# Modulation rows in column strips, one block of a product moved, gelu groups dealt out again, scaled rows stored from another queue

## The chip, the cores and the metric

The kernel runs on one core of a Trainium2 chip. The metric is the device time of one execution in microseconds (us). A core has five engines with instruction streams of their own: TensorE (PE, matrix products), VectorE (DVE), ScalarE (ACT), GpSimd (POOL) and SyncE (SP, which here only starts transfers). Transfers (DMA) are started from the queues of SP, POOL and ACT.

## The reference

The program computes a block with adaptive layer norm, forward and backward (2048 tokens, model width 1024, hidden width 3584, bfloat16 in and out):

```python
mod = (silu(c) @ w_mod).reshape(1, 6, 1, -1)      # six rows of 1024
sa, ca, ga, sb, cb, gb = mod[:, 0], ..., mod[:, 5]
h = layernorm(x) * (1 + ca) + sa
x = x + ga * irfft2(rfft2(h) * (w_r + 1j * w_i))
h = layernorm(x) * (1 + cb) + sb
x = x + gb * (gelu(layernorm(h) @ w1 + b1) @ w2 + b2)
```

Returned are the result (out_0) and, for a given gradient of it, the gradients of x, w_r, w_i, w1 (out_4), b1, w2, b2, c and w_mod (out_9, 1024 x 6144: column block r is silu(c) as a column times the gradient of row r).

## The kernel before, in words

**Stages.** The program runs once through these stages, on a span of 1370.3 us. First come the modulation rows, the layer norm of x and its fold for the Fourier transform; at the same time PE computes blocks of ph = (gb * grad_out) w2^T, the gradient of the hidden layer. Then comes the forward Fourier stage (matrix products with generated cosines), whose last part also makes the layer norms of the MLP. After it the rest of ph, the MLP forward with its gelu (here from some 300 us), then the gradients of w2, of the hidden layer, the backward Fourier stage, and last the gradient of w1.

**Modulation rows.** `mod_block(r, h)` (L277) computes half h (512 columns) of row r on all 128 partitions at once: eight matmuls (L283) of 128 x 512 whose left operand `u_b` holds silu(c) 128 times over, each adding 128 rows of w_mod, and then a cast out of PSUM (L286) on whichever engine the scheduler picks. Rows 1 and 5 are made earlier; the change touches rows 0, 2, 3 and 4, eight halves. They are issued in three groups (2, 3 and 3 halves) inside the loop over early ph blocks (L934). Row 0 (`saf` after a scaling and a fold) is added to the folded x at the end of the first stage (`fbuf<-fbuf,sb_saf`, DVE).

**ph blocks.** ph has 28 blocks `fc` of four parts of eight matmuls (`ph_part`, L543, matmul at L548); each part is cast out of PSUM by `ph_out` (L540) into `pho` or `phr` and stored. `PH_EARLY` = 10 sets how many are computed ahead of the Fourier stage (block 10 is the last), the rest but four half blocks (from `PH_KEEP` = 24) after it, the second halves of those at the head of the MLP plan.

**Layer norm of the MLP.** For each quarter i of the tokens (tiles `xt`, `ct`) DVE or ACT makes mean and variance; `ln_fin` (L473) takes a square root on ACT and a reciprocal on DVE (L475), and the rows are normalised on DVE (L507) or ACT (L514).

**Gelu groups and passes.** The MLP runs over four token blocks b of 512. `z_block(b, g)` makes a group of four hidden chunks: 32 matmuls (L1076, `pz`), four evictions with the bias on ACT (L1079), and the gelu with its derivative: a square (L1083) and two sigmoids (L1087, L1089) on ACT, nine products on DVE. The first of its results is hh (tiles `hhA`, `hhB`, `hhC`, made by `hh<-gt,gt`), written hh0, hh1, ... by the group's number 7b + g. Work tiles `gt` are held in two sets that the groups use in turn. A pass of the second product (`bo_pass`, 16 matmuls at L1130, `pbo`) uses hh of one group with a block of w2; each b has 14 passes, two per group, so pass k of b = 0 is the first to need hh of group k for k under 7. At L1119 four matmuls of one row and at L1149 four matmuls into 32 partitions each start side by side (`tile_position` and partition ranges).

**What sets the order.** A scheduler places every engine's instructions in one list ahead of time, by its own cost estimates and by priorities (`tc.high_priority()`). PE's order at these places is fixed by hand: `ordered()` ties a matmul to the one before, and the list `plan` (L1166) with its table `Z_AT` says in which order gelu groups ("z"), the kept ph halves ("p") and passes ("b") follow one another. `issue_after` and `behind` hold an instruction behind another in the list.

**The last stage.** `gw1_quads` computes the gradient of w1 in four quads c; each finished tile `gwo` is stored to out_4 (L1681), the first eleven of them from POOL's queue, later ones from SP's. Between them `gmod_scaled` (L1291) makes 32 pieces of out_9, each one activation on ACT (L1298, into one of five tiles `otl`) and one store of 256 KB (L1299). The loop at L1858 takes one such step per quarter of a quad and two in its last nine.

Of the kernel before, what the change touches and what calls it, by code (L numbers as in the profile page):

```python
# [17 lines left out]
P = 128  # L18
# [17 lines left out]
def kernel(  # L36
# [36 lines left out]
    def ps_s(name):  # L73
        return psum.tile([P, 512], FP32, tag="s", name=name)
# [191 lines left out]
    def mod_tile():  # L266
        wring[0] += 1
        return reg.tile([P, NDC, KH], BF16, name="wblk", tag=PXT[3 + wring[0] % 3])

    def mod_load(r, h, wblk, eng, parts=1):  # L270
        cb = 2 * r + h
        src = w_mod[:, cb * KH:(cb + 1) * KH].rearrange("(j p) n -> p j n", p=P)
        for k in range(parts):
            js = slice(k * NDC // parts, (k + 1) * NDC // parts)
            eng.dma_start(out=wblk[:, js, :], in_=src[:, js, :])

    def mod_block(r, h, wblk=None):  # L277
        if wblk is None:
            wblk = mod_tile()[:]
            mod_load(r, h, wblk, nc.sync)  # L280
        pm = (ps_s, ps_d)[wring[0] % 2]("pm")
        for jc in range(NDC):
            nc.tensor.matmul(pm[:], lhsT=u_b[:, jc, :], rhs=wblk[:, jc, :], start=(jc == 0), stop=(jc == NDC - 1))  # L283
        dst = MOD_DST[r][:, h * KH:(h + 1) * KH]
        with tc.high_priority():
            nc.any.tensor_copy(out=dst, in_=pm[:])  # L286
        if r in (1, 4):
            nc.vector.tensor_scalar(out=dst, in0=dst, scalar1=1.0, scalar2=None, op0=ALU.add)

    def fold_d(dst, src, tmp):  # L290
# [237 lines left out]
    def ordered():  # L528
        return tc.issue_after(last_pe[0].ins)

    PH_EARLY, PH_KEEP = 10, NFC - 4

    def ph_out(fc, j, pp):
        ph2 = phs[fc % 4]
# [9 lines left out]
    def ph_part(fc, js):  # L544
        for j in js:
            pp = ps_f("pp")
            for cch in range(NDC):
                last_pe[0] = nc.tensor.matmul(pp[:], lhsT=wt[:, fc % 4, cch, :], rhs=gBoT[j][:, cch, :],  # L548
                                              start=(cch == 0), stop=(cch == NDC - 1))
            ph_out(fc, j, pp)  # L550
# [377 lines left out]

    phs.append(reg.tile([P, 4, BW], BF16, name="phr", tag="ph")[:])

    late_mods = [(r, h) for r in (2, 3, 4) for h in range(2)]
    for fc in range(PH_EARLY):
        if fc > 1:
            ph_part(fc, (0, 1, 2, 3))  # L934
        load_w2t(fc + 4)
        if fc == 4:
            with ordered():
                small_rows()
        if fc == 3:
            for h in range(2):  # L940
                with ordered():
                    mod_block(0, h)
            nc.vector.tensor_scalar(out=sar[:, 0], in0=sar[:, 0], scalar1=8.0, scalar2=None, op0=ALU.mult)
            fold_d(saf.rearrange("p (c d) -> p c d", c=1), sar[:, 0], sar[:, 1])
        if fc in (5, 7):
            with ordered():
                for r, h in late_mods[3 * (fc // 2 - 2):3 * (fc // 2 - 1)]:
                    mod_block(r, h)

    ph_part(PH_EARLY, (0, 1, 2, 3))  # L950
    early_pe = last_pe[0]
# [61 lines left out]
    for fc in range(PH_EARLY + 1, NFC):  # L1013
        if fc >= PH_EARLY + 4:
            load_w2t(fc)
            load_w1({14: 2, 27: 5}.get(fc, 0))
# [150 lines left out]
    Z_AT = [{1: ((0, 4),), 2: ((0, 5),), 3: ((0, 6),), 4: ((1, 0),), 6: ((1, 1),), 7: ((1, 2),), 9: ((1, 3),), 10: ((1, 4),),  # L1167
             11: ((1, 5),), 12: ((1, 6),)}]
    Z_AT += [{k: ((b, g),) for g, k in enumerate((0, 2, 4, 7, 9, 11, 12))} for b in (2, 3)] + [{}]
    for b in range(NB):  # L1170
        for k in range(14):
            plan += [("z",) + bg for bg in Z_AT[b].get(k, ())] + [("b", b, k)]
    boq = {}
    for kind, b, g in plan:
        if kind == "z":
# [117 lines left out]
    def gmod_scaled(rows):  # L1293
        for n in range(len(rows) * NDC):
            k, jc = n // NDC, n % NDC
            gw, r = w1g["gw"][n % 5], rows[k]
            with tc.issue_after(w1g["ev"].ins):
                nc.scalar.activation(out=gw, in_=w1g["gr"][k], func=ACT.Identity, scale=u_rt[:, jc:jc + 1])  # L1298
            nc.gpsimd.dma_start(out=out_9[jc * P:(jc + 1) * P, r * D:(r + 1) * D], in_=gw)  # L1299
            yield  # L1300

    step_in = []
# [607 lines left out]
```

## Time and profile before

| what | value |
|---|---|
| median of 3 runs | 1375.88 us (1375.06 to 1378.72) |
| the profiled execution's own time | 1372.29 us |
| its span, first to last instruction | 1370.3 us |
| granted PE clock, mean | 0.997 |
| busy: PE, DVE, ACT, POOL | 1345.6, 1077.2, 792.4, 390.3 us |
| HBM traffic over the span | 205 GB/s |

All positions in the trace count from the start of the span. The profiled execution is one run, 3.6 us under the median of the three timed ones; differences between two kernels are worked out against its own time and then carried to the median. Busy time is the sum over an engine's instructions; a row of a group gives busy time, mean length in ns, and the idle time ahead with what ended it.

### The profile page before, as it was taken

Reading aid. Unit: us, or ns where it says so; the run is one execution under the profiler, and the core shown is the slowest. Engines: PE = TensorE matmul, PEld = TensorE weight load, DVE = VectorE, ACT = ScalarE, POOL = GpSimd, SP = SyncE. Lnnn points to the kernel's source line nnn. Section 1 sums busy time; section 2 is a strip of 40 time slices with the busy share of each in tenths; the row PEclk is TensorE's granted clock in tenths of the full one; section 3 lists DMA queues with packets and bytes.
Section 4 is the critical chain, followed back from the end, with each engine's and each line's share of the span. In section 5 each row is a group of like instructions: output and inputs, shape, how many; then the busy total and the mean of one; then the engine's idle time right before and its main releaser. Section 6 shows DMA issues by size and latency. Waiting matters only on the chain. (4 is left out here: it accounts for less than half of the span.)

```text
span 1370.3 us, 18631 instructions
## 1 busy us (share of the span) xinstructions
PE 1345.6 (98%) x6899; PEld 651.0 (48%) x6899; DVE 1077.2 (79%) x1467; ACT 792.4 (58%) x1120; POOL 390.3 (28%) x436
## 2 busy tenths in 40 slices
PE   7999999999999999999999999999999999999997
PEld 4445566444444444444444444444644555444443
DVE  6997889999988878787620578889888488976985
ACT  4864667767877765665414593445732554544456
POOL 6273642411112122212211010112344330332163
PEclk9999999999999999999999999999999999999999
DMA  9975594899787887698999699988579878899876
GB/s 326 322 196 140 160 256 154 250 279 318 262 254 252 212 261 246 199 289 233 284 278 224 181 217 311 296 254 257 179 238 270 222 160 237 207 245 251 201 271 244
DMA packets 356401, 330.08 MB, mean 241 GB/s; under 512 B 203866, under 2 KB 298736, under 8 KB 356182
## 3 DMA queue, kind: packets, MB, share of 16 engines
q1 hardware_dynamic: 314310, 201.02, 57.2%
q0 software_dynamic: 35232, 120.00, 26.0%
q10 hardware_dynamic: 6768, 7.87, 1.7%
q8 instruction: 54, 0.88, 0.3%
q14 instruction: 37, 0.30, 0.1%
HBM read 165.73 MB, written 114.87 MB: 205 GB/s over the span
## 5 line engine op out<-in xcount | busy, mean ns | idle before, releaser
L1230 PE MATMUL pg<-w1T,gzr 128*128 128x512 bf16 x896 | 195.8, 380 | 0.0
L548 PE MATMUL pp<-gBoT,wt 128*128 128x512 bf16 x832 | 185.4, 379 | 3.2 <-ACT pho L540 1.9
L1076 PEld LDWEIGHTS <-w 128*128 128x128 bf16 x896 | 87.2, 98 | 107.4 <-issue 2.9
L1230 PEld LDWEIGHTS <-gzr 128*128 128x128 bf16 x896 | 86.5, 98 | 108.5 <-issue 5.8
L548 PEld LDWEIGHTS <-wt 128*128 128x128 bf16 x832 | 81.0, 98 | 97.9 <-issue 5.3
L1770 PE MATMUL gw1acc<-gzh,n3n 128*128 128x512 bf16 x512 | 111.8, 380 | 0.0
L1076 PE MATMUL pz<-n3Ta,w 128*128 128x512 bf16 x448 | 98.8, 380 | 1.4 <-ACT gt L1079 1.4
L1076 PE MATMUL pz<-n3Tb,w 128*128 128x512 bf16 x448 | 99.0, 380 | 0.0
L1770 PEld LDWEIGHTS <-n3n 128*128 128x128 bf16 x640 | 62.3, 98 | 76.7 <-issue 3.1
L195 DVE TENSOR_TENSOR ct<-ct 128x2048 bf16<-128x2048 bf16 (+1 forms) x84 | 91.5, 1120 | 4.3 <-ACT n L514 2.0
L1079 ACT ACTIVATE gt<-pz,b_col 128x512 bf16<-128x512 f32 x112 | 72.8, 682 | 37.3 <-PE pz L1076 33.1
L1130 PEld LDWEIGHTS <-hhA 128*128 128x128 bf16 x608 | 58.9, 98 | 73.2 <-issue 3.0
L1087 ACT ACTIVATE gt<-gt 128x2048 bf16<-128x2048 bf16 x28 | 53.5, 1911 | 58.3 <-DVE gt L195 58.3
L1411 PE MATMUL gw2acc<-gB,hhsA 128*128 128x512 bf16 x384 | 84.8, 380 | 0.0
L195 DVE TENSOR_TENSOR gt<-gt,gt 128x2048 bf16<-128x2048 bf16 x56 | 68.4, 1223 | 17.7 <-ACT gt L1089 16.8
L1419 ACT CAST gwo<-gw2acc 128x512 bf16<-128x512 f32 x40 | 23.5, 588 | 87.5 <-PE gw2acc L1411 84.2
L1411 PEld LDWEIGHTS <-hhsA 128*128 128x128 bf16 x384 | 37.5, 98 | 43.5
L1083 ACT ACTIVATE gt<-gt 128x2048 bf16<-128x2048 bf16 x28 | 53.4, 1908 | 3.1 <-DVE hhC L195 2.4
L540 ACT CAST pho<-pp 128x512 bf16<-128x512 f32 x68 | 38.6, 584 | 27.3 <-PE pp L548 24.1
L1774 ACT CAST gwo<-gw1acc 128x512 bf16<-128x512 f32 x40 | 23.0, 579 | 53.6 <-PE gw1acc L1770 41.6
L1089 ACT ACTIVATE gt<-gt 128x2048 bf16<-128x2048 bf16 x28 | 53.3, 1905 | 0.3
L1411 PE MATMUL gw2acc<-gB,otl 128*128 128x512 bf16 x224 | 50.0, 380 | 0.0
(414 smaller groups left out, 2710.3 us busy)
## 6 DMA issues: line engine op xcount, KB each, us to landing
gzr<-d_gz SPq DMA_DIRECT2D x28, 512.0 KB
d_ph<-pho POOLq DMA_DIRECT2D x21, 512.0 KB, 5.5
wblk<-in_w_mod_dram SPq DMA_DIRECT2D x10, 1024.0 KB
out_dram<-otl POOLq DMA_DIRECT2D x40, 256.0 KB, 4.1
d_hh<-hhA POOLq DMA_DIRECT2D x19, 512.0 KB, 5.6
wrw<-in_w_mod_dram SPq DMA_DIRECT2D x32, 256.0 KB
w<-in_B_w_dram SPq DMA_DIRECT2D x7, 1024.0 KB
hhC<-d_ph SPq DMA_DIRECT2D x14, 512.0 KB
```

What stands on the lines that cost most here:

```text
L195: return nc.vector.tensor_tensor(out=out, in0=a, in1=b, op=op)
L540: copy(out=ov, in_=pv)
L548: last_pe[0] = nc.tensor.matmul(pp[:], lhsT=wt[:, fc % 4, cch, :], rhs=gBoT[j][:, cch, :], start=(cch == 0), stop=(cch == NDC - 1))
L1076: last_pe[0] = nc.tensor.matmul(pz[:], lhsT=w1s[g][:, cch, k * P:(k + 1) * P], rhs=n3T[:, cch, :], start=(cch == 0), stop=(cch == NDC - 1))
L1079: z_in = nc.scalar.activation(out=zb[:, k, :], in_=pz[:], func=ACT.Identity, bias=b1_col[:, fc:fc + 1], scale=1.0)
L1083: nc.scalar.activation(out=av, in_=zb, func=ACT.Square)
L1087: nc.scalar.activation(out=sg, in_=bv, func=ACT.Sigmoid, scale=2.0 * GK)
L1089: nc.scalar.activation(out=bv, in_=bv, func=ACT.Sigmoid, scale=-2.0 * GK)
L1130: last_pe[0] = nc.tensor.matmul(pbs[i][:], lhsT=hh[:, k, i * P:(i + 1) * P], rhs=wp[:, k, :], start=False, stop=(g == 6 and k == 3))
L1230: last_pg[0] = nc.tensor.matmul(pgs[i][:], lhsT=gzs[b, g][:, k, i * P:(i + 1) * P], rhs=w1Ts[g][:, k, h * KH:(h + 1) * KH], start=(g == 0 ...
L1411: nc.tensor.matmul(acc[:], lhsT=hh_of(fc)[:, t, :], rhs=gBs[t // 4][:, t % 4, h * KH:(h + 1) * KH], start=(t == 0), stop=(t == NT - 1))
L1770: nc.tensor.matmul(acc[:], lhsT=n3ns[t // 4][:, t % 4, cch * P:(cch + 1) * P], rhs=gz2[t // 8][:, t % 8, :], start=(t == 0), stop=(t == NT ...
```

## The change

Four edits:

1. The halves of rows 0, 2, 3 and 4 are computed in strips. A group of 2 or 3 halves shares one PSUM bank: half k goes to partitions 32k to 32k + 31, by matmuls with 32 columns of `u_b` on the left, so eight steps of 2 or 3 matmuls. ACT casts the bank once into bf16 (L308 in the new numbering). Two parts of the next ph block later, one matmul per half with a single row on the left (L314) spreads the row over 128 partitions again, and ACT casts that to its destination (L318). The loads of w_mod for the second and third group are issued one step earlier.
2. `PH_EARLY` is 11: one more ph block is computed ahead of the Fourier stage, one fewer after it. The third group of modulation rows moves from block 7 to block 8.
3. The plan has two gelu groups behind the kept ph halves instead of three, and the following 25 groups are dealt over the passes by one table.
4. The 32 stores of out_9's scaled pieces are issued from ACT's queue instead of POOL's, and two steps are taken per quarter from the seventh on, instead of in the last nine.

Lines of the new kernel lie 36 to 37 below those of the old from there on (L540 is L576, L473 is L509, L1079 is L1116).

```diff
+    def mod_strips(rows, wblks):
+        pm = ps_s("pm")
+        for jc in range(NDC):
+            for k in range(len(rows)):
+                with ordered():
+                    last_pe[0] = nc.tensor.matmul(pm[32 * k:32 * (k + 1), :], lhsT=u_b[:, jc, 0:32], rhs=wblks[k][:, jc, :],
+                                                  start=(jc == 0), stop=(jc == NDC - 1))
+        n = 32 * len(rows)
+        with tc.high_priority():
+            nc.scalar.copy(out=strips[0:n, :], in_=pm[0:n, :])
+
+        def spread():
+            for k, (r, h) in enumerate(rows):
+                pr = (ps_d, ps_s)[k % 2]("pr")
+                with ordered():
+                    last_pe[0] = nc.tensor.matmul(pr[:], lhsT=ones_bf[32 * k:32 * k + 1, :], rhs=strips[32 * k:32 * k + 1, :],
+                                                  start=True, stop=True, tile_position=(32 * k, 0))
+                dst = MOD_DST[r][:, h * KH:(h + 1) * KH]
+                with tc.high_priority():
+                    nc.scalar.copy(out=dst, in_=pr[:])
...
-    PH_EARLY, PH_KEEP = 10, NFC - 4
+    PH_EARLY, PH_KEEP = 11, NFC - 4
...
         if fc > 1:
-            ph_part(fc, (0, 1, 2, 3))
+            ph_part(fc, (0, 1))
+            if spread is not None:
+                spread = spread()
+            ph_part(fc, (2, 3))
...
         if fc == 3:
-            for h in range(2):
-                with ordered():
-                    mod_block(0, h)
...
+            spread = mod_strips(*mod_loads([(0, 0), (0, 1)]))
+            late_in = mod_loads(late_mods[0:3])
+        if fc in (5, 8):
+            spread = mod_strips(*late_in)
+            if fc == 5:
+                late_in = mod_loads(late_mods[3:6])
...
-    plan = [("z", 0, 0)] + [("p", fc, 0) for fc in range(PH_KEEP, NFC)] + [("z", 0, 1), ("z", 0, 2), ("z", 0, 3)]
-    Z_AT = [{1: ((0, 4),), 2: ((0, 5),), 3: ((0, 6),), 4: ((1, 0),), 6: ((1, 1),), 7: ((1, 2),), 9: ((1, 3),), 10: ((1, 4),),
...
+    plan = [("z", 0, 0)] + [("p", fc, 0) for fc in range(PH_KEEP, NFC)] + [("z", 0, 1), ("z", 0, 2)]
+    Z_AT = (1, 2, 3, 4, 6, 8, 9, 11, 13, 15, 16, 18, 20, 22, 23, 25, 27, 28, 30, 32, 34, 35, 37, 39, 41)
...
-            nc.gpsimd.dma_start(out=out_9[jc * P:(jc + 1) * P, r * D:(r + 1) * D], in_=gw)
+            nc.scalar.dma_start(out=out_9[jc * P:(jc + 1) * P, r * D:(r + 1) * D], in_=gw)
...
-        for _ in range(2 if n >= left - 9 else 1):
+        for _ in range(2 if n >= 6 else 1):
             next(scaled, None)
```

**What stands where.** ACT, first stage, around the generated cosines (`smB<-gidx`), before:

```order
L418 ACT_TABLE_LOAD
L418 ACTIVATE smax<-gidx,negpi 128x1024 x2
L418 ACTIVATE smB<-gidx_269,negpi 128x1024 x2
L418 ACTIVATE smB<-smax,negpi 128x1024
L608 ACTIVATE al<-genv 128x2 x2
L418 ACTIVATE smB<-gidx,negpi 128x1024
L473 ACT_TABLE_LOAD
```

and now:

```order
L454 ACT_TABLE_LOAD
L454 ACTIVATE smax<-gidx,negpi 128x1024 x2
L454 ACTIVATE smB<-gidx_269,negpi 128x1024 x2
L454 ACTIVATE smB<-smax,negpi 128x1024
L308 CAST sar<-pm 64x512
L454 ACTIVATE smB<-gidx,negpi 128x1024
L576 CAST pho<-pp 128x4x128
L644 ACTIVATE al<-genv 128x2 x2
L509 ACT_TABLE_LOAD
L509 ACTIVATE mv<-mv,eps_c 128x4
L318 CAST sar<-pr 128x512 x2
```

The cast of the first strips (L308) stands behind five sine activations, and the two casts of the spread row 0 (L318) behind a table load and a square root.

ACT at the entry into the MLP, last layer norms and first gelu groups, before:

```order
L514 ACTIVATE ct<-ct,stats 128x1024 x4
L500 ACTIVATE ct,mv<-xt,mv 128x1024
L993 DMA d_n_99<-ct 128x4x1024
L473 ACTIVATE mv<-mv,eps_c 128x4
L1083 ACTIVATE gt_3116<-gt_3116 128x2048
L514 ACTIVATE ct<-xt,stats 128x1024 x2
L1087 ACT_TABLE_LOAD
L1087 ACTIVATE gt_3117<-gt_3117 128x2048
```

and now:

```order
L509 ACTIVATE mv<-mv,eps_c 128x4
L1124 ACT_TABLE_LOAD
L1124 ACTIVATE gt_3131<-gt_3131 128x2048
L550 ACTIVATE ct<-ct,stats 128x1024 x4
L1116 ACTIVATE gt_3277<-pz,b_col 128x512
L1030 DMA d_n_99<-ct 128x4x1024
L1116 ACTIVATE gt_3277<-pz,b_col 128x512 x3
L509 ACT_TABLE_LOAD
L509 ACTIVATE mv<-mv,eps_c 128x4
```

The sigmoid of the first gelu group (L1087, now L1124) and four evictions of the second have moved ahead of the next-to-last square root (L473, now L509), and with them two table loads.

DVE at the same place, up to the first group's hh, before:

```order
L195 TENSOR_TENSOR ct<-ct,sb_saf 128x4096
L1090 TENSOR_SCALAR gt_3116<-gt_3116 128x2048
L483 BN_STATS st<-ct 128x6 x3
L484 BN_AGGR mv<-st 128x2
L483 BN_STATS st<-ct 128x6 x2
L484 BN_AGGR mv<-st 128x2
L483 BN_STATS st<-ct 128x6 x2
L484 BN_AGGR mv<-st 128x2
L483 BN_STATS st<-ct 128x6
L195 TENSOR_TENSOR hhB<-gt_3117,gt_3116 128x2048
```

and now:

```order
L1127 TENSOR_SCALAR gt_3130<-gt_3130 128x2048
L576 CAST phr<-pp 128x4x128
L530 BN_AGGR mv<-st 128x2
L195 TENSOR_TENSOR hhB<-gt_3131,gt_3130 128x2048
L531 TENSOR_SCALAR mv<-mv 128x2
L511 RECIPROCAL stats<-mv 128x4
L195 TENSOR_TENSOR stats<-mv,stats 128x4
L543 TENSOR_SCALAR ct<-xt,stats 128x1024 x2
L195 TENSOR_TENSOR ct<-ct,rows_87 128x4096
L195 TENSOR_TENSOR ct<-ct,sb_saf 128x4096
```

The last quarter's normalisation, its two products and its statistics stood ahead of hh0 and now stand behind it.

POOL, the last rows of the program, before:

```order
L1681 DMA out_dram<-gwo_9683 128x512
L1299 DMA out_dram<-otl 128x1024 x3
L1681 DMA out_dram<-gwo_9683 128x512
L1299 DMA out_dram<-otl 128x1024 x8
L1905 UNCONDITIONAL_BRANCH
```

and now:

```order
L1810 DMA out_dram<-gwo_9697 128x512 x10
L167 DMA out_dram<-ct,xu 2048x1024 x2
L1810 DMA out_dram<-gwo_9697 128x512 x10
L1716 DMA out_dram<-gwo_9697 128x512 x11
L1940 UNCONDITIONAL_BRANCH
```

The stores of out_9's pieces (L1299) are gone from there; the eleven stores of out_4 (L1681, now L1716) are POOL's last.

More of the change, by code (lines that the diff above doesn't have):

```diff
@@ L288, in mod_block, with mod_loads @@
             nc.vector.tensor_scalar(out=dst, in0=dst, scalar1=1.0, scalar2=None, op0=ALU.add)
+    strips = sarx[:, 2 * D + KH:3 * D]
+    def mod_loads(rows):
+        wblks = []
+        for r, h in rows:
+            wblks.append(mod_tile()[:])
+            mod_load(r, h, wblks[-1], nc.sync)
+        return rows, wblks
+    def mod_strips(rows, wblks):
[17 more added lines that the diff above has]
+                    nc.scalar.copy(out=dst, in_=pr[:])
+                if r == 4:
+                    nc.vector.tensor_scalar(out=dst, in0=dst, scalar1=1.0, scalar2=None, op0=ALU.add)
+            if rows[0][0] == 0:
+                nc.vector.tensor_scalar(out=sar[:, 0], in0=sar[:, 0], scalar1=8.0, scalar2=None, op0=ALU.mult)
+                fold_d(saf.rearrange("p (c d) -> p c d", c=1), sar[:, 0], sar[:, 1])
+        return spread
     def fold_d(dst, src, tmp):
@@ L929 @@
     phs.append(reg.tile([P, 4, BW], BF16, name="phr", tag="ph")[:])
+    spread = None
     late_mods = [(r, h) for r in (2, 3, 4) for h in range(2)]
@@ L1015 @@
             load_w2t(fc)
-            load_w1({14: 2, 27: 5}.get(fc, 0))
+            load_w1({15: 2, 27: 5}.get(fc, 0))
         if fc == N3_AT:
@@ L1164 @@
     bo_late = []
-    plan = [("z", 0, 0)] + [("p", fc, 0) for fc in range(PH_KEEP, NFC)] + [("z", 0, 1), ("z", 0, 2), ("z", 0, 3)]
-    Z_AT = [{1: ((0, 4),), 2: ((0, 5),), 3: ((0, 6),), 4: ((1, 0),), 6: ((1, 1),), 7: ((1, 2),), 9: ((1, 3),), 10: ((1, 4),),
-             11: ((1, 5),), 12: ((1, 6),)}]
-    Z_AT += [{k: ((b, g),) for g, k in enumerate((0, 2, 4, 7, 9, 11, 12))} for b in (2, 3)] + [{}]
+    plan = [("z", 0, 0)] + [("p", fc, 0) for fc in range(PH_KEEP, NFC)] + [("z", 0, 1), ("z", 0, 2)]
+    Z_AT = (1, 2, 3, 4, 6, 8, 9, 11, 13, 15, 16, 18, 20, 22, 23, 25, 27, 28, 30, 32, 34, 35, 37, 39, 41)
     for b in range(NB):
         for k in range(14):
-            plan += [("z",) + bg for bg in Z_AT[b].get(k, ())] + [("b", b, k)]
+            plan += [("z", n // 7, n % 7) for n, at in enumerate(Z_AT, 3) if at == 14 * b + k] + [("b", b, k)]
     boq = {}
```

6 lines of the change are left out of this document (removed).

## The prediction

> **What bounds the kernel now.** The page's first part comes first.
>
> ```profile
> PE 1345.6 (98%) x6899; PEld 651.0 (48%) x6899; DVE 1077.2 (79%) x1467; ACT 792.4 (58%) x1120; POOL 390.3 (28%) x436
> ```
>
> PE is busy for 98% of the span of 1370.3 us, so over the whole program only fewer matmuls, fewer PE waits or a shorter end can help. Next, the waits of PE, with total, count and longest:
>
> ```profile
> PE pp L548 <- ACT pho L540: 1.9, 2, 1.7
> PE pz L1076 <- ACT gt L1079: 1.4, 1, 1.4
> PE pp L548 <- DVE pho L540: 1.2, 2, 0.7
> ```
>
> Little is left to win there directly. But an average hides stages, and the change works in two of them, so I read busy time by stretch (length, then PE, PEld, DVE, ACT, POOL, clock, DMA share, GB/s):
>
> ```profile
> 42.00:119.00 77.00, 74.66 (x346) 33.58 (x344) 76.66 (x115) 53.35 (x71) 45.68 (x29) 1.00 0.77 230
> 203.00:250.00 47.00, 47.00 (x299) 28.98 (x297) 46.23 (x50) 35.05 (x64) 19.29 (x14) 1.00 0.53 175
> 250.00:300.00 50.00, 49.82 (x255) 23.42 (x254) 45.84 (x77) 33.82 (x56) 9.63 (x12) 1.00 0.85 252
> 300.00:350.00 50.00, 47.89 (x224) 21.30 (x222) 46.80 (x70) 36.56 (x44) 9.12 (x11) 1.00 0.97 317
> 350.00:395.00 45.00, 45.00 (x210) 20.39 (x209) 41.94 (x45) 38.60 (x36) 7.15 (x9) 1.00 0.80 261
> ```
>
> From 42 to 119 us DVE has 0.3 us free, and from 203 to 395 it is busy for 180.8 of 192 us. In both stretches PE only just doesn't wait for DVE. PE time removed ahead of 395 us is a gain only if DVE's results come earlier too. What DVE waits for from 203 to 395 us, the three largest:
>
> ```profile
> DVE mv L501 <- ACT ct L500: 2.9, 1, 2.9
> DVE ct L195 <- ACT n L514: 2.0, 1, 2.0
> DVE ct L195 <- ACT ct L514: 1.8, 1, 1.8
> ```
>
> These 6.7 us are all that DVE could gain, and each ends with a piece of ACT's work.
>
> **Modulation rows.** The 64 matmuls of L283 become 64 strip matmuls, each set on 2 or 3 of the array's column strips, and 8 spreads. The group of L283 from 55 to 125 us, the issue interval of such matmuls, strips that exist already (L1149), and the one-row matmuls of L1119, each with what follows:
>
> ```profile
> L283 PE MATMUL pm<-wblk,u_b 128*128 128x512 bf16 x64 | 14.3, 380 | 0.0
> 101.14 20.88 PE L548 MATMUL pp<-gBoT,wt 128*128 128x512 bf16 x96
> 421.36 0.40 PE L1149 MATMUL pa<-otile,ones_bf 128*32 128x512 bf16 x4
> 421.69 2.55 PE L1076 MATMUL pz<-n3Tb,w 128*128 128x512 bf16 x11
> 347.98 0.40 PE L1119 MATMUL pbo<-b_row,ones_bf 1*128 1x512 bf16 x4
> 348.30 3.63 PE L1130 MATMUL pbo<-w2sA,hhB 128*128 128x512 bf16 x16
> ```
>
> Matmuls start every 20.88/96 = 0.217 us, so 64 take 13.9. Four strips and the way back to full width take 421.69 − 421.36 = 0.33 us, so a set runs side by side. Eight sets in a row cost at least 8 × 0.217 = 1.74 and, if each paid for its way in and out, 8 × 0.33 = 2.6. I take 1.74 plus two changes of 0.1 (0.33 less 0.217), 1.9, since within a group no full-width matmul comes between; three groups make 5.8 (up to 7.9). Spreads: 0.32 for four by L1119, 1.3 for three groups with 0.1 in and out, at most 8 × 0.217 = 1.7. PE saves 13.9 − 7.1 = 6.8 (at least 4.3).
>
> The eleventh block of w2^T takes 32 × 0.217 = 6.9 us of that place again. So early PE time stays as it is (+0.1), and the block's 6.9 are missing later.
>
> The spread is a new wait: its PE matmul needs ACT's cast of the strips (L308). The order with the change shows that cast behind five sine activations; they now run here (start, length), and PE's first group of modulation rows there:
>
> ```profile
> 56.56 3.62 PE L283 MATMUL pm<-wblk,u_b 128*128 128x512 bf16 x16
> 57.36 1.28 ACT L418 ACT_TABLE_LOAD   x1
> 62.83 1.13 ACT L418 ACTIVATE smB<-smax,negpi 128x1024 bf16<-128x1024 int32 x1
> ```
>
> ACT is free at 63.9 and the cast done at 64.4 (0.58 by casts of that size), while PE, two parts (16 × 0.217 = 3.5) after strips that end at 56.56 + 1.9 = 58.5, asks at 62.0. All following blocks are queued on PE behind the spread: about 2.4 us of wait, once. DVE is the bound here, and it wants work only by the order: 18 casts of L540 for 14, two of L286 for five, one cast of some 0.6 more. I put the end of the fold at +0.6: between −2.2 (were the eleven ACT casts worth four on DVE) and +4 (the whole wait, and 1.6 more by which DVE's casts then come late).
>
> **Entry into the MLP.** By the new plan PE comes to the second w2 pass without the block (6.9), without one gelu group (6.9) and, stall-free, without the waits of 1.4 and 0.7 quoted above. PE now:
>
> ```profile
> 340.98 7.07 PE L1076 MATMUL pz<-n3Ta,w 128*128 128x512 bf16 x32 [1.44 <-ACT gt L1079]
> 358.68 3.62 PE L1130 MATMUL pbo<-w2sC,hhB 128*128 128x512 bf16 x16
> 362.13 7.07 PE L1076 MATMUL pz<-n3Ta,w 128*128 128x512 bf16 x32
> 403.57 3.62 PE L1130 MATMUL pbo<-w2sD,hhA 128*128 128x512 bf16 x16
> ```
>
> So it wants the second pass's operand (hh1) at 358.68 − 15.9 = 342.8. DVE now, with the durations needed below:
>
> ```profile
> 325.31 0.68 DVE L540 CAST pho<-pp 128x512 bf16<-128x512 f32 x1
> 338.38 0.64 DVE L483 BATCH_NORM_STATS2 st<-ct 128x6 f32<-128x512 bf16 x1
> 338.94 1.21 DVE L195 TENSOR_TENSOR hhB<-gt,gt 128x2048 bf16<-128x2048 bf16 x1
> 347.09 1.22 DVE L195 TENSOR_TENSOR hhB<-gt,gt 128x2048 bf16<-128x2048 bf16 x1
> 393.86 1.23 DVE L195 TENSOR_TENSOR hhA<-gt,gt 128x2048 bf16<-128x2048 bf16 x1 [1.25 <-ACT gt L1087]
> ```
>
> hh0 is done at 340.1, hh1 at 348.3, hh6 at 395.1. In the two orders DVE has the same instructions ahead of hh1 (those of the last layer-norm step stand behind hh0 now, ahead of it before). So hh0 comes much earlier, but hh1 where it was, moved only by DVE's idle time. ACT decides that:
>
> ```profile
> L514 ACT ACTIVATE ct<-ct,stats 128x1024 bf16<-128x1024 bf16 x4 | 4.6, 1230 | 0.1
> L1079 ACT ACTIVATE gt<-pz,b_col 128x512 bf16<-128x512 f32 x31 | 19.4, 678 | 4.9 <-DVE hhB L195 3.7 <-PE pz L1076 1.1
> 327.29 1.28 ACT L1087 ACT_TABLE_LOAD   x1
> 328.59 1.91 ACT L1087 ACTIVATE gt<-gt 128x2048 bf16<-128x2048 bf16 x1
> ```
>
> With the change the next-to-last square root stands on ACT, counted from the one before, behind a table load, a sigmoid, four normalisations, four evictions and a table load: 1.28 + 1.91 + 4 × 1.23 + 4 × 0.68 + 1.28 + 0.3 for itself = 12.4. DVE covers that with four statistics, three casts, two products of 0.68 and 1.21 and small rows, about 7.3. It waits 5.1 where now 2.9 stand, so +2.2: hh1 at 348.3 + 0.6 + 2.2 = 351.1. From there to the seventh pass PE has five passes of 3.45 (362.13 − 358.68) and four groups of 6.91, 44.9 us; I add 1.0 for waits on the last square root and on evictions (0 to 2.1): 397.0. One gelu group is then still owed against before: 397.0 + 6.9 = 403.9, against 403.57 now. Up to here the change brings **+0.4**. Ends: if all 6.7 us of DVE's waits went, hh6 would come at 395.1 + 0.6 − 6.7 = 389.0 and PE stand at 395.9, −7.7; upwards +7.7, worked out with the third rival.
>
> The Trainium skill ("ScalarE: Activation LUTs", What ACT_TABLE_LOAD costs) gives a switch 1.28 us of load and 1.38 of drain. The rows above agree with the load and not with the drain: the sigmoid starts 1.30 after its load began. By the page hh1 would come 2.8 later, as an estimate, and the sum would rise by as much.
>
> Later gelu groups stand on PE ahead of passes that have the same 3.45 us each; nothing shows a wait there, so nothing is taken.
>
> **The end.** The last transfers and the last stretches:
>
> ```profile
> 1351.28 0.54 POOL L1681 DMA_DIRECT2D out_dram<-gwo  x1
> 1362.75 0.54 POOL L1299 DMA_DIRECT2D out_dram<-otl  x1 [0.49 <-ACT otl L1298]
> 1365.00:1366.00 1.00, 0.00 (x0) 0.00 (x0) 0.00 (x0) 0.00 (x0) 0.00 (x0) 0.86 0.31 108
> 1367.00:1370.30 3.30, 0.00 (x0) 0.00 (x0) 0.00 (x0) 0.00 (x0) 0.00 (x0) 0.50 0.00 0
> SPq L1905 <- PEq L1905: 4.0, 2, 3.5
> ```
>
> Bytes stop near 1365.3, yet the span runs to 1370.3, and SP's last line waits 3.5 us for the other engines. What is in use as late is POOL's store queue, until 1362.75; with the change POOL's last store is the last of out_4 there (L1681 in the first row), 1362.75 − 1351.28 = 11.5 us earlier. I take the wait as POOL's and give **−3.3** (0 to −3.5). ACT gets 32 issues, at most POOL's 0.54 us each, 17 in all. ACT is busy for 58% of the span, and scaling and issuing are spread over more steps of the last stage, so ACT's free time hides them and I cost them at nothing; were it used up, what PE waits for on ACT, the casts of L1676 among others, would come late by a part of the 17.
>
> Sum: +0.4 − 3.3 = −2.9. Against the profiled execution's 1372.29 that is 1369.4; the median of the runs, 1375.88, stands 3.6 above that execution, so 1373.0 is forecast. What differs from before by under 0.3%, 4.1 us, counts as no change.
>
> **Rivals.** *DVE comes earlier* (0.37): with the strips' casts on ACT and less gelu work ahead, half of DVE's 6.7 us of waits goes. hh1 at 345.5, hh6 at 392.3 sets the seventh pass, plus 6.9 makes 399.2: −4.4, with the end −7.7, 1368.2. For it: each of those waits is short. Against it: two more table loads in the order.
>
> *The end stays* (0.08): those 3.5 us belong to the program's end whatever queue was used, 1376.3. The row names PE, not POOL, which speaks for it; that it is one long wait after the last byte speaks for a queue. The Trainium skill ("DMA: Bandwidth & Descriptors", Issuing engines are not separate DMA queues) says that another issuing engine saves only the sequencer's time to start a transfer; by that rule this is the result.
>
> *ACT becomes the bound* (0.17): the spread's wait reaches the fold in full (+4), and the square root ahead of hh1 adds its 5.1 to DVE's old waits instead of replacing one, so hh1 comes at 348.3 + 4 + 5.1 = 357.4 and the seventh pass, plus what is owed, at 357.4 + 44.9 + 2.1 + 6.9 = 411.3, +7.7. With the end −3.3 that is +4.4, 1380.3. It decides from hh1 later than about 357. For it: ACT is at 38.6 of 45 us from 350 to 395. Against it: ACT is at 53 of 77 early.
>
> *The strips run one after another* (0.02): 64 × 0.217 as before plus the spreads, +8, 1381. The 0.33 us speaks against it.
>
> **How the numbers follow.** My own forecast has the remaining 0.36 and reaches from 1370 to 1376. Faster gets the first rival and a little of mine, 0.39; slower the third and fourth, 0.19; no change 0.42. The range takes in both large rivals, from 1365 (DVE's waits nearly gone, −7.7 − 3.3) to 1381.
>
> **What would show it.** L283 replaced by strips that take 2 us a group; PE waiting for ACT's cast near 62; hh1 near 351 with PE waiting some 8 us ahead of the second pass; two more table loads; the stretch after the last byte shorter by 3.3. Wrong if PE reaches the second pass unheld, or if a wait of several us appears in the later passes or in the last 90 us.

## The result and the profile after

The changed kernel takes 1388.82 us (median of 5 runs, 1386.43 to 1392.29), the kernel before 1375.06 on the same chip (5 runs): 1.0102 times as long, 95% interval 1.0082 to 1.0123. It is slower by 1.0%; forecast were 1373 us, and a range from 1365 to 1381. Its profiled execution took 1386.43 us with a span of 1384.6, so against the profile of before there are 14.3 us of span to explain. First its busy times, then the five of PE's waits on DVE and ACT that bear on the change:

```profile
PE 1337.6 (97%) x6780; PEld 648.1 (47%) x6907; DVE 1078.5 (78%) x1468; ACT 799.6 (58%) x1124; POOL 368.7 (27%) x404
```

```profile
PE pbo L1167 <- DVE hhB L195: 7.0, 1, 7.0
PE gw1acc L1805 <- ACT gwo L1809: 3.8, 1, 3.8
PE pbo L1167 <- DVE hhA L195: 2.9, 2, 1.6
PE gqy L1721 <- ACT snap L1703: 1.8, 1, 1.8
PE pr L314 <- ACT sar L308: 1.3, 1, 1.3
```

(Some 130 matmul records are missing from this trace, so PE's busy time is not to be compared.) Of the first four, before had only the second, with 1.5 us instead of 3.8 and at a later place. DVE is busy for 1.3 us more than before and ACT for 7.2 of some 800. So the change made PE wait more than it made any engine work.

Next PE at the entry into the MLP, where before it came from the first pass to the seventh without a wait:

```profile
336.39 3.41 PE L1167 MATMUL pbo<-w2sA,hhB 128*128 128x512 bf16 x15
339.86 7.07 PE L1113 MATMUL pz<-n3Ta,w 128*128 128x512 bf16 x32
353.92 5.15 PE L1167 MATMUL pbo<-w2sC,hhB 128*128 128x512 bf16 x16 [7.00 <-DVE hhB L195]
358.91 7.07 PE L1113 MATMUL pz<-n3Ta,w 128*128 128x512 bf16 x31
365.82 3.62 PE L1167 MATMUL pbo<-w2sD,hhC 128*128 128x512 bf16 x16
...
377.93 3.63 PE L1167 MATMUL pbo<-w2sB,hhA 128*128 128x512 bf16 x16 [1.59 <-DVE hhA L195]
...
393.20 3.63 PE L1167 MATMUL pbo<-w2sC,hhA 128*128 128x512 bf16 x15 [1.28 <-DVE hhA L195]
...
403.57 3.62 PE L1167 MATMUL pbo<-w2sD,hhA 128*128 128x512 bf16 x15
407.12 1.64 PE L1156 MATMUL pbo<-b_row,ones_bf 1*128 1x512 bf16 x4
```

The first pass starts at 336.4, 11.9 us earlier than before. Then PE stands for 7.0 us until hh1 is there at 353.9, and the pass after it takes 5.15 us where all others take 3.6. The seventh pass starts at 403.57, to the hundredth where it stood before, but with one gelu group less behind PE. A half block is seven passes that add into the same four PSUM banks. In the last row the second half block starts directly behind a pass, and its four one-row matmuls take 1.6 us until the next pass instead of 0.33: they wait, bank by bank, for ACT's evictions of the first half. Two later half blocks start the same way, at 461 and 515 us. Ahead of those passes the old plan had a gelu group.

ACT and DVE at the same place:

```profile
320.40 0.29 ACT L509 ACTIVATE mv<-mv,eps_c 128x4 f32<-128x4 f32 x1
320.71 1.28 ACT L1124 ACT_TABLE_LOAD   x1
322.00 1.91 ACT L1124 ACTIVATE gt<-gt 128x2048 bf16<-128x2048 bf16 x1
323.82 4.62 ACT L550 ACTIVATE ct<-ct,stats 128x1024 bf16<-128x1024 bf16 x4
328.35 0.67 ACT L1116 ACTIVATE gt<-pz,b_col 128x512 bf16<-128x512 f32 x1
...
330.76 1.28 ACT L509 ACT_TABLE_LOAD   x1
332.06 0.30 ACT L509 ACTIVATE mv<-mv,eps_c 128x4 f32<-128x4 f32 x1
```

```profile
DVE stats L511 <- ACT mv L509: 5.9, 2, 4.9
DVE ct L195 <- ACT ct L550: 3.1, 2, 1.8
```

From the end of one square root (320.69) to the end of the next (332.36) ACT needs 11.7 us, and DVE waits 4.9 of them.

The end:

```profile
1380.00:1381.00 1.00, 0.94 (x5) 0.21 (x3) 0.00 (x0) 0.02 (x1) 0.00 (x0) 1.00 0.19 64
1382.00:1384.60 2.60, 0.00 (x0) 0.00 (x0) 0.00 (x0) 0.00 (x0) 0.00 (x0) 0.97 0.35 128
```

Bytes still move in the last stretch. The last matmul ends at 1380.9, so 3.6 us follow it, against 7.2 before (1363.1 to 1370.3).

Six places of the program and the span, as the difference to the trace of before in us. The columns are traces of one execution each: after, and the experiments below (e1 old plan, e2 ten blocks, e3 queue alone, e4 groups at halves, e5 strips alone, e6 stores early on POOL, e7 stores back, e10 less DVE, e11 first twelve stores on POOL).

| place (start in before) | after | e1 | e2 | e3 | e4 | e5 | e6 | e7 | e10 | e11 |
|---|---|---|---|---|---|---|---|---|---|---|
| last transposed piece of grad_out (35.4) | +1.4 | +1.6 | +3.3 | −0.3 | +3.0 | +1.1 | +5.1 | +0.7 | +1.1 | +3.1 |
| first Fourier matmul (121.9) | +1.5 | +1.3 | −5.1 | +1.2 | +1.1 | +0.5 | +3.4 | +3.2 | +3.2 | +1.0 |
| first gelu group (304.0) | −4.8 | −5.2 | +1.9 | +1.3 | −5.5 | +2.1 | +3.5 | −4.1 | −4.1 | +1.1 |
| first matmul behind the MLP (715.0) | +11.3 | +6.1 | +9.3 | −0.1 | +13.9 | +6.1 | +2.0 | +10.9 | +5.5 | +0.9 |
| first quad (1314.3) | +15.9 | +7.0 | +19.4 | +1.7 | +17.8 | +4.5 | +0.3 | +10.0 | +7.8 | −0.8 |
| end of the last matmul (1363.1) | +17.8 | +15.6 | +26.8 | +11.2 | +24.9 | +4.5 | +0.3 | +10.0 | +16.8 | −0.8 |
| span (1370.3) | +14.3 | +12.5 | +23.3 | +8.1 | +21.4 | +4.5 | −3.3 | +9.2 | +13.3 | −4.7 |

The first row lies ahead of everything that the change touches: it differs by up to 5 us between traces, with the transfers of the start. So a trace is read by the differences from one row to the next, and medians of different calls only beside the kernel before of the same call.

For the changed kernel that gives: 1.4 at the start, 1.2 more up to the last step of the forward Fourier stage (L874), 8.7 from there to the end of the MLP (−6.9 for the block that moved; 15.6 of waits and slow matmuls more than before), 4.6 from there to the quads (a transfer and ACT, a wait of 3.8 among them), 1.9 in the quads, and −3.5 at the end: 14.3.

### The profile page after: what moved, and what is told of

The parts are those of the page before. It is cut to its first block, busy times and chain, and to the rows that moved or that the text cites. A ratio compares the mean times of both kernels' runs of the same rounds, so it can differ in the third digit from the quotient of the medians.

```text
span 1384.6 us, 18496 instructions
## 1 busy us (share of the span) xinstructions
PE 1337.6 (97%) x6780; PEld 648.1 (47%) x6907; DVE 1078.5 (78%) x1468; ACT 799.6 (58%) x1124; POOL 368.7 (27%) x404
## 5 line engine op out<-in xcount | busy, mean ns | idle before, releaser
L1116 ACT ACTIVATE gt<-pz,b_col 128x512 bf16<-128x512 f32 x112 | 73.8, 684 | 55.6 <-PE pz L1113 53.0
L1124 ACT ACTIVATE gt<-gt 128x2048 bf16<-128x2048 bf16 x28 | 53.5, 1909 | 48.8 <-DVE gt L195 48.4
L576 ACT CAST pho<-pp 128x512 bf16<-128x512 f32 x64 | 36.7, 585 | 27.2 <-PE pp L584 26.7
```

Source lines behind the costliest of these rows:

```text
L1116: z_in = nc.scalar.activation(out=zb[:, k, :], in_=pz[:], func=ACT.Identity, bias=b1_col[:, fc:fc + 1], scale=1.0)
L1124: nc.scalar.activation(out=sg, in_=bv, func=ACT.Sigmoid, scale=2.0 * GK)
```

## The experiments

### The old plan

```diff
-    plan = [...] + [("z", 0, 1), ("z", 0, 2)]
-    Z_AT = (1, 2, 3, 4, 6, 8, 9, 11, 13, ...)
+    plan = [...] + [("z", 0, 1), ("z", 0, 2), ("z", 0, 3)]
+    Z_AT = [{1: ((0, 4),), 2: ((0, 5),), ...}]
...
```

> The changed kernel with the old plan of gelu groups (three groups behind the kept halves, a group ahead of the first pass of each half block). Theory: most of the loss is the new plan. It asks for hh1 some 16 us earlier than before, of which PE waited 7.0 us in the changed kernel and then ran at half clock for 3.3 us (1.6 us lost), and at three starts of a half block no group stands ahead of the pass, so that its four first matmuls wait for ACT's evictions (1.25 us each). Expected: the wait for hh1 falls under 3 us, the three starts take 0.33 us again instead of 1.57, median some 10 to 14 us below the changed kernel, 1375 to 1379. Rival: the loss sits in the first stage and in ACT's new casts; then this kernel stays within 3 us of the changed one, 1386 to 1391.

Median 1385.8 (before 1375.4), ratio 1.0071 (1.004 to 1.0103): hardly better, so the median expected, 1375 to 1379, was missed. The three starts of half blocks take 0.33 us again, but PE waits at another place:

```profile
342.97 3.63 PE L1167 MATMUL pbo<-w2sA,hhB 128*128 128x512 bf16 x16
354.70 7.55 PE L1113 MATMUL pz<-n3Ta,w 128*128 128x512 bf16 x24 [8.10 <-ACT gt L1116]
```

```profile
350.36 1.91 ACT L1124 ACTIVATE gt<-gt 128x2048 bf16<-128x2048 bf16 x1 [8.76 <-DVE gt L195]
353.98 2.40 ACT L1116 ACTIVATE gt<-pz,b_col 128x512 bf16<-128x512 f32 x4
```

The wait for hh1 is gone because PE stands earlier: 8.1 us ahead of the fifth gelu group, for evictions (the second row of ACT) that are queued behind a sigmoid, which waits 8.8 us for DVE. So the plan does not make the wait, it only chooses where PE meets it. Up to the end of the MLP the trace is 5.2 us better than the changed kernel's; in the quads it is 6.7 worse, which the expectation had not foreseen either.

### Ten early blocks

```diff
-    PH_EARLY, PH_KEEP = 11, NFC - 4
+    PH_EARLY, PH_KEEP = 10, NFC - 4
...
-            load_w1({15: 2, 27: 5}.get(fc, 0))
+            load_w1({14: 2, 27: 5}.get(fc, 0))
```

> The changed kernel with ten early blocks of w2^T instead of eleven. Theory: DVE sets the end of the first stage, so PE, with the strips' 6.8 us saved and nothing put in their place, waits some 5 to 7 us ahead of the first Fourier matmul; the block is computed later and the wait for hh1 (7.0 us and 1.6 of half clock) goes. Expected: within 3 us of the changed kernel, 1385 to 1390. Rival: the eleventh block is what delays DVE's fold and the entry; then the first Fourier matmul starts earlier by some us and the median falls to about 1380.

Median 1387.2, ratio 1.0083 (1.0052 to 1.0114). PE reaches the first Fourier matmul 5.1 us earlier than before, in spite of a start that is 3.3 late. That is 8.4 us, of which 1.5 are waits that the trace of before had on the way (2.2 against 0.7), so the strips do save PE about the 6.8 forecast. Then it waits (three of PE's waits in this trace):

```profile
PE pu L675 <- DVE fbuf L195: 4.7, 1, 4.7
PE pu L675 <- ACT U L942: 2.6, 1, 2.6
PE pbo L1167 <- DVE hhA L195: 3.4, 2, 3.0
```

4.7 us go to the fold. Behind that wait fourteen matmuls of 256 columns start 0.21 us apart instead of 0.11, and at the last matmul of this kind (132.3 us in before) the trace is 0.5 us late, at the first gelu group 1.9. The saved PE time is lost before it leaves the first stages. (The second row lies far behind, in the backward Fourier stage at 985 us.) The theory holds as to DVE. The wait for hh1 went too, but not the loss up to the end of the MLP (+9.3): PE waits for later hh instead, and three starts of half blocks take 1.6 to 1.8 us here as well.

### The stores alone on ACT's queue

```diff
-            nc.gpsimd.dma_start(out=out_9[...], in_=gw)
+            nc.scalar.dma_start(out=out_9[...], in_=gw)
...
-        for _ in range(2 if n >= left - 9 else 1):
+        for _ in range(2 if n >= 6 else 1):
```

> The kernel before with only the out_9 stores on ACT's queue and two steps per quarter from the seventh on. Theory: the idle stretch at the end shrinks by 3.6 us as in the changed kernel, and ACT's extra work in the quads costs PE one wait of about 1.8 us at a quad's start: median 1.5 to 3.6 us below before, 1371.5 to 1373.5. Rival: the shorter end of the changed kernel comes from something else, or ACT's 32 issues cost as much as the end gives: 1375 or more.

Median 1378.7, ratio 1.0017 (0.9993 to 1.0041): not faster, and in its trace 8.1 us longer. The end is shorter, as in the changed kernel, but PE stands in the first quads (waits of PE, of ACT from 1290 to 1330 us, and of SP's queue there):

```profile
PE gqy L1686 <- ACT snap L1668: 7.0, 1, 7.0
```

```profile
ACT gwo L1774 <- DMA d_gmod<-row: 7.7, 1, 7.7
ACT gwo L1774 <- DMA wrw<-in_w_mod_dram: 3.1, 1, 3.1
```

```profile
SPq L201 <- DVE row L200: 12.6, 1, 12.6
```

ACT's cast of a finished tile is put down to transfers that it doesn't use. The trace's own events show why (start in us, engine, semaphore):

```
1304.49  SP   starts to wait, d_gmod<-row (L201), semaphore 105
1317.13  SP   transfer d_gmod<-row issued,        semaphore 105
1318.26  ACT  wait on semaphore 105 ends
1318.32  ACT  transfer out_dram<-otl (L1299) issued, semaphore 105
1318.75  ACT  cast gwo<-gw1acc (L1774)
```

A transfer of ACT's queue uses a completion semaphore that a transfer of SP's queue had last, and ACT waits until that one has landed. SP's transfer stood 12.6 us for DVE, ACT with it for 7.7 of them, and behind ACT's issue stood the casts and snapshots that PE needs. The stretch from the first quad to the last matmul is longer by 0.7 to 9.5 us in the eight traces with all 32 stores on ACT's queue (1.9 in that of the changed kernel, where ACT waited 2.9 and 2.8 us for the same two kinds of transfer of SP's queue just before).

### Stores early, but on POOL's queue

```diff
-        for _ in range(2 if n >= left - 9 else 1):
+        for _ in range(2 if n >= 6 else 1):
```

> The kernel before with only the number of scaling steps changed (two per quarter from the seventh on), stores still on POOL's queue. Theory: with the stores on ACT's queue an issue waits there for the landing of an earlier store, and ACT's casts that PE waits for are behind it (the 7.0 us wait at the first quads); on POOL's queue nothing else waits. Expected: no wait of several us of PE at the quads, the idle stretch at the end about as short as in the changed kernel since POOL's last transfer comes some 10 us earlier; 2 to 4 us below before in the trace, median 1371 to 1374. Rival: the wait at the quads comes from two steps per quarter (ACT's activations, five buffers), not from the queue; then it is there too, and the median is 1376 to 1380.

Median 1370.0 against 1373.0, ratio 0.9985 (0.9963 to 1.0007). No wait in the quads: from the first quad to the last matmul nothing is added, and the end is 3.5 us instead of 7.2. So in this trace the steps are harmless, and the end shrinks without ACT's queue. Repeated:

> The kernel with stores on POOL's queue but two steps per quarter from the seventh on, again, in five rounds: its end was 3.6 us shorter in the trace and its interval reached from 0.37% faster to 0.07% slower. Theory: 3 to 4 us faster than before, ratio 0.997 to 0.998 with an interval that leaves out 1. Rival: what the end gives is within the spread of the runs: interval around 1.

1372.6 against 1373.3, ratio 0.9993 (0.9976 to 1.0009): the expectation missed. The end was short again (3.5 us), but by the median the 3.6 us gained there cannot be told from no change. Nor are the steps always harmless: in this trace ACT waits 4.0 us at the first quads until a store has landed and given its tile `otl` back, PE waits 1.1 for ACT, and the stretch from the first quad to the last matmul is 1.5 us longer. Ahead of the quads this kernel runs the instructions of before in the same order on every engine, yet two waits stand between MLP and quads to which the account of the prediction comes back:

```profile
DVE ct L195 <- DMA out_dram<-ct: 7.0, 1, 7.0
PE gw1acc L1770 <- ACT gwo L1774: 2.2, 1, 2.2
```

The first quad is 4.0 us later against the end of the MLP than in the trace of before; in the first trace of this kernel it was 1.7 earlier.

### The first twelve stores on POOL's queue, the others on ACT's

```diff
-            nc.gpsimd.dma_start(out=out_9[...], in_=gw)
+            (nc.scalar if n >= 12 else nc.gpsimd).dma_start(out=out_9[...], in_=gw)
```

together with two steps from the seventh quarter on, in the kernel before.

> The kernel before with two scaling steps per quarter from the seventh on, the first 12 stores of out_9 on POOL's queue and the other 20 on ACT's. Theory: PE's 7.0 us at the first quads come from ACT's issues that wait there for completion semaphores last given to SP's queue, whose store of a gradient row (d_gmod, L201) waits 12.6 us for DVE; the later issues on ACT find theirs free. Expected: no wait of over 2 us of PE at the first quads, the end as short as with all stores early on POOL's queue, 1368 to 1373. Rival: any stores on ACT's queue hold its casts up: 5 us or more of PE waits in the later quads, 1374 or more.

Median 1369.9 against 1373.3, ratio 0.9978 (0.9958 to 0.9998): the only version here whose interval lies below 1, by a little. The first quads in busy time, with all stores on ACT's queue, and with the first twelve on POOL's (PE is the first figure behind the length):

```profile
1318.00:1324.00 6.00, 1.70 (x8) 0.68 (x7) 2.54 (x6) 2.67 (x3) 0.54 (x1) 1.00 0.70 198
1324.00:1330.00 6.00, 3.33 (x8) 1.13 (x8) 3.35 (x6) 4.24 (x5) 1.08 (x2) 0.56 0.63 224
```

```profile
1318.00:1324.00 6.00, 6.00 (x30) 2.73 (x28) 4.94 (x8) 4.44 (x6) 2.15 (x4) 1.00 0.83 288
1324.00:1330.00 6.00, 6.00 (x30) 2.70 (x29) 3.81 (x9) 4.86 (x6) 1.08 (x2) 1.00 0.94 311
```

In this trace twenty stores on ACT's queue cost PE nothing; it was the first ones, issued while SP's queue stood, that did.

### All stores back

```diff
-            nc.scalar.dma_start(out=out_9[...], in_=gw)
+            nc.gpsimd.dma_start(out=out_9[...], in_=gw)
...
-        for _ in range(2 if n >= 6 else 1):
+        for _ in range(2 if n >= left - 9 else 1):
```

> The changed kernel with part 4 undone: stores on POOL's queue, two steps only in the last nine quarters. Theory: PE's waits in the quads (1.9 us in the changed kernel's profile, 7 to 9 in four others with its stores on ACT's queue) go and the idle stretch of 3.6 us at the end comes back: 0 to 5 us below the changed kernel, 1384 to 1388, and still 9 to 12 above before. Rival: the whole loss is the queue; then it comes back to 1375 to 1379.

Median 1383.9 against 1373.0, ratio 1.008 (1.0052 to 1.0109), as the theory had it: most of the loss is not the queue. PE waits 7.0 us for hh1 as in the changed kernel, the end of the MLP is 10.9 late, and 6.4 us follow the last matmul again.

### Groups at the starts of half blocks

```diff
-    Z_AT = (1, 2, 3, 4, 6, 8, 9, 11, 13, 15, 16, 18, 20, 22, 23, ...)
+    Z_AT = (1, 2, 3, 4, 7, 8, 9, 11, 14, 15, 16, 18, 21, 22, 23, ...)
```

> The changed kernel with three gelu groups moved so that one stands ahead of the first pass of each half block (passes 7, 14 and 21 instead of 6, 13 and 20). Theory: the four one-row matmuls run side by side again there, 0.33 us instead of 1.57 at each of three places: 3.7 us less, about 1385. Rival: the 1.57 us are only shifted to another wait and the median stays at 1388 to 1389.

Median 1392.8, ratio 1.0117 (1.0076 to 1.0158): the rival was right about the waits, and the median lies above what it had (four runs, 1387.6 to 1394.8). The one-row matmuls take 0.33 us again, but the pass ahead of the moved group now meets a DVE that is not done:

```profile
392.47 3.63 PE L1167 MATMUL pbo<-w2sC,hhA 128*128 128x512 bf16 x16 [1.28 <-DVE hhA L195]
399.27 5.10 PE L1167 MATMUL pbo<-w2sD,hhA 128*128 128x512 bf16 x16 [3.18 <-DVE hhA L195]
411.21 0.39 PE L1156 MATMUL pbo<-b_row,ones_bf 1*128 1x512 bf16 x4
```

3.2 us for hh6 and 1.5 of slow matmuls replace the 3.7.

### DVE's work taken away

```diff
-        tt(tmp, tmp, bcn(opcb_row, 4), ALU.mult)
-        tt(tmp, tmp, bcn(sb_row, 4), ALU.add)
+        if i < 3:
+            tt(tmp, tmp, bcn(opcb_row, 4), ALU.mult)
+            tt(tmp, tmp, bcn(sb_row, 4), ALU.add)
```

> The changed kernel without the two row products (times 1 + cb, plus sb) of the last quarter of the tokens: that part of the computation is left out, 2 x 2.3 us of DVE between hh0 and hh1. Theory: DVE's queue of work sets hh1 (353.9 in the changed kernel), so hh1 comes 4 to 5 us earlier, PE's wait for it shrinks from 7.0 to 2 to 3 us, and with it the half-rate matmuls (1.6 us) go: the sixth half block starts 5 to 7 us earlier against the same place of the changed kernel. Rival: ACT's square roots and evictions set hh1: it moves by less than 1.5 us, and PE's wait stays over 5.

```profile
348.90 3.63 PE L1168 MATMUL pbo<-w2sC,hhB 128*128 128x512 bf16 x16 [1.28 <-DVE hhB L195]
```

The last quarter of the tokens goes without these two products; the kernel ran once. 4.6 us less on DVE make the second pass start 5.0 us earlier (353.92 to 348.90); the wait falls to 1.3, the pass takes 3.63 again, and the MLP ends 5.8 us earlier (+5.5 instead of +11.3). DVE's list of work is what PE waits for at the entry. (The span is hardly shorter, 1383.6, since in this trace the stores on ACT's queue held the quads up by 9.0 us.)

### The strips alone

The kernel before with `mod_strips` in place of `mod_block`, third group at block 7 as before; nothing else.

> The kernel before with the strips alone: ten early blocks, old plan, stores on POOL's queue as before. Theory: PE saves 6.8 us ahead of the fold, but DVE decides when the fold ends and when hh1 to hh6 come; with ten blocks the fold comes earlier by 2 to 3 us (seen with ten blocks in the changed kernel) and a part of that reaches the end. Expected: PE reaches the first Fourier matmul 3 to 6 us earlier, a wait on fbuf or U there, median 1370 to 1377. Rival: the strips with their spreads and ACT casts are themselves a loss (their wait for ACT, the later square roots), 1378 to 1385.

Median 1378.8 against 1373.0, ratio 1.0051 (1.0033 to 1.007): the rival's side. PE reaches the first Fourier matmul 0.5 us late instead of 3 to 6 early. But not for the rival's reason alone:

```profile
93.61 0.38 PE L304 MATMUL pm<-wblk,u_b 128*32 128x512 bf16 x1 [0.46 <-DMA wblk<-in_w_mod_dram]
97.76 2.57 PE L304 MATMUL pm<-wblk,u_b 128*32 128x512 bf16 x18 [3.77 <-DMA wblk<-in_w_mod_dram]
```

With PE ahead of its time, the third group's rows of w_mod are not there yet: 4.2 us, and 1.9 more for ACT's cast ahead of the first spread. That eats the 6.8 in the first stage; at the entry into the MLP ACT stands in another order and PE waits 4.2 us for evictions there, 1.4 before, with 1.4 of slow matmuls behind the longer wait.

### The wait filled

Twenty-four matmuls without use ahead of the second pass, first into a bank of the gelu groups, then (32 x 512, with zeros) into the banks of the running pass.

> The changed kernel with 24 more matmuls of 128 x 512 (5.2 us) into an unused bank ahead of the second pass, in PE's wait of 7.0 us for hh1; their result is used by nothing. Theory: the eleven matmuls after a wait of 7 us run at half rate because PE stood idle; kept busy, the pass takes 3.5 us instead of 5.2, and nothing is lost by the 5.2 us of added work: the start of the third w2 pass comes 1.5 us earlier in the trace, median 0 to 2 us below the changed kernel. Rival: the half rate has another cause (the operand, the bank, transfers): the pass still takes 5.2 us.

This missed: the bank that I took was waiting for an eviction of the fourth gelu group, PE stood 8.1 us ahead of the added matmuls, and nothing could be read. Median 1387.5, ratio 1.0104 (1.006 to 1.0148).

> The changed kernel with 24 matmuls of 32 x 512 (5.2 us) that add zeros to the banks of the running pass, ahead of the second w2 pass, in PE's wait for hh1; unlike the try before, they need no bank that waits for an eviction. Theory: eight matmuls after the wait of 7.0 us run at half rate because PE stood idle; with 1.8 us of idle time left they don't: the 16 matmuls of the pass take 3.5 us instead of 5.2, and the third pass starts 1.5 us earlier (364.3 instead of 365.8) although 5.2 us of work were added. Rival: the half rate comes from the operand or the transfers: the pass still takes 5.2 us and the third starts no earlier.

```profile
344.88 5.35 PE L1170 MATMUL pbo<-n3Ta,zero 128*32 128x512 bf16 x24
351.94 3.63 PE L1174 MATMUL pbo<-w2sC,hhB 128*128 128x512 bf16 x16 [1.71 <-DVE hhB L195]
355.40 7.07 PE L1113 MATMUL pz<-n3Ta,w 128*128 128x512 bf16 x32
363.29 3.63 PE L1174 MATMUL pbo<-w2sD,hhC 128*128 128x512 bf16 x16 [0.81 <-DVE hhC L195]
```

The kernel ran once. With 5.35 us of work in the wait, the pass takes 3.63 us instead of 5.15. The slow matmuls come from PE standing. But this whole trace runs 2.0 us ahead of the changed kernel's at the first gelu group, so the third pass gains only 0.5 us of the 1.5 expected: PE now waits 0.8 for hh2. DVE sets that, too.

## Why the prediction was wrong

**What held.** The strips: a set of 16 matmuls takes 2.4 us (58.05 to the next block at 60.41) against 1.9, the spread of two 0.32, and with ten blocks PE came to the Fourier stage earlier by about the 6.8 forecast, once the waits on the way are counted. The wait of PE for ACT's cast near 62: 1.3 us against 2.4. The square root's distance on ACT: 11.7 against 12.4, and DVE's wait 4.9 against 5.1. hh1 at 353.9 against 351.1, of which 1.4 was late from the start. PE's wait ahead of the second pass: 7.0 against some 8. The end: 3.5 us shorter against 3.3, and with stores early on POOL's queue it shrank just as much, so it goes with POOL's last store, as taken. The trace shows what stands behind that store: a DRAIN of POOL, which before runs from 1362.73 to 1369.49, close to the end of the span, and in the changed kernel from 1369.38 to 1374.11, some ten us ahead of it.

**What failed.** The step from hh1 to the end of the MLP, "from there to the seventh pass PE has ... 44.9 us; I add 1.0", and "later gelu groups ...; nothing shows a wait there, so nothing is taken". Four terms were missing or too small: the slow matmuls after the wait (1.5), the waits for hh3 and hh5 (2.9 against 1.0), hh1 itself (2.8 later, half of it from the start), and three starts of half blocks without a group ahead (1.24 each, 3.7). The seventh pass, with the group still owed, stood at 403.57 + 6.9 = 410.5 against 403.9 forecast, and the half blocks added the rest. The last term could be read from the plan: passes 7, 14 and 21, counted from 0, have no group in the new table.

Taken together, the sum had −2.9 us and the span grew by 14.3. Of the 17.2 between them 9.5 arise up to the end of the MLP (11.3 less the 0.4 forecast and the 1.4 of the start), 1.9 in the quads, 4.6 between MLP and quads and 1.4 at the start, less 0.2 at the end.

The second step that failed is "ACT's free time hides them and I cost them at nothing". The 32 issues cost little of ACT's time, but they make ACT wait for transfers of SP's queue: the quads are 1.9 us longer in the profile of the changed kernel, 0.7 to 9.5 in others. I had asked what is queued behind ACT's instruction and had not asked what the issue itself waits for.

The 4.6 us between MLP and quads have another source: ACT's casts there came late behind DVE, which waited 9.2 us for a store of out_1 to land where before it waited 3.3. In the trace with the stores back it waited 7.0, and PE for ACT 0.6 instead of 3.8. The second trace with stores early on POOL's queue shows that it comes without the change: with the order of before up to the quads, DVE waited 7.0 us for that store there, PE 2.2 for ACT, and the quads began 4.0 later. So a delay of this size differs from execution to execution, and how much of the 4.6 the change adds, if any, stays open. The 2.4 us by which the median lies above the profiled execution are no loss of the change either: before, the median lies 2.8 above (1375.06 to 1372.29).

**The rivals.** *ACT becomes the bound* had the direction and named the entry, but its price rested on a fold 4 us late, which was 0.4 late beyond the start. *DVE comes earlier* asked for hh1 at 345.5, and it came at 353.9. *The end stays* was wrong by 3.5 us, and *the strips run one after another* by the 2.4 us that 16 of them took (one after another, 3.5). What decided was DVE's list with ACT's square root in it, and PE's own recovery after the wait. That DVE bounds both stretches was read rightly; I then forecast that waits would about balance the saving, while long waits bring a further cost.

## What to carry to other kernels

Time saved on the busiest engine is worth nothing where another engine's list sets the next operand: ask for the operand's time in the new order, and take every place at which PE would come earlier as a wait until shown otherwise. A wait of several us can be dearer than its length, and a reordering that takes it away in one place can hand it to the next pass, as the old plan and the groups at half blocks showed here. Before a transfer is moved to another engine's queue, look at what its issue waits for there and at what stands behind it; by the medians, twelve of 32 stores left where they were stand between 0.2% slower and 0.2% faster, at the border of what these runs can tell apart.

## What was not expected of the hardware

After PE has stood for several us its matmuls can run at half rate. After the wait of 7.0 us starts lie 0.427 us apart instead of 0.216 for seven matmuls, and the granted clock falls in the profile's stretches:

```profile
346.00:354.00 8.00, 1.00 (x6) 0.28 (x4) 7.63 (x10) 3.30 (x2) 0.77 (x1) 0.76 0.10 34
354.00:358.00 4.00, 4.00 (x12) 1.49 (x13) 2.90 (x3) 3.98 (x6) 0.77 (x1) 0.62 0.85 264
```

After waits of 3.8 us and more in different kernels it lasts 3 to 5 us and costs 1.4 to 2.4 us. After waits of 1.3 to 1.8 us starts stay 0.216 apart. In between both are seen: after 2.1 us starts stay 0.216 apart in one trace, and in another (the wait filled with zeros, at 375.9 us) slow matmuls follow a little later and cost 1.6; after 3.4 us, with ten early blocks at 1263.6 us, none is slow. That the clock stayed up when the same wait was filled shows the cause. The Trainium skill ("TensorE: Matmul & The Clock Gate", Part 1: The HAM clock gate) says that an idle window of about 3.4 us halves the clock and that as long a busy one brings it back, the windows running free of the program. The traces agree for waits of 3.8 us and more. That slow matmuls followed waits of 2.1 and 2.2 us too does not fit a whole window of idle time, and there the measurement stands. I had the rule at hand and did not apply it to the wait of 8 us that I forecast. And in this program transfers of SP's and ACT's queues use the same completion semaphores (105 in the events above): an engine that starts a transfer can wait for another engine's transfer that has nothing to do with it, ACT here for 7.7 us.
